# One stored batch of X instead of two: attention of odd batches split, w_out decoded later, GpSimd in pieces

## The chip, the cores and the metric

The kernel runs on one core of one Trainium2 chip. The metric is the device time of one execution in microseconds, as the median of several runs. Engines are named as in the profile: PE is TensorE's matrix multiplication and PEld its weight load, DVE is VectorE, ACT is ScalarE, POOL is GpSimd, SP is SyncE, which issues all DMAs here. "L227" is line 227 of the kernel.

## The reference

A linear attention without a softmax, normalised per head, feeds a gated block with a spatial mixing matrix. B = 8 batches, 8 heads, S = 576 positions, head size 64, d_model = 512, d_ff = 1024; everything is float32.

```python
kv  = einsum('bhsd,bhse->bhde', k, v)
o   = einsum('bhsd,bhde->bhse', q, kv)
x   = o / sqrt(mean(o*o, -1) + 1e-6) * g_norm          # then (b, s, h*d): 576 x 512
h   = maximum(x @ w_in, 0);  u, v = h[..., :512], h[..., 512:]
v_n = (v - mean(v)) / sqrt(var(v) + 1e-6)
v_s = einsum('ts,bsd->btd', w_spatial, v_n) + b_spatial[None, :, None]
out = (u * v_s) @ w_out
```

## The kernel before, in words

**Precision.** Products other than the attention's are made from high and low parts: a value is rounded to fp32r (the high part) and the rest is kept as a second fp32r tile, and each product is the sum of three matmuls, high x high, high x low and low x high (`hl`, `three`, L227). So there are pairs of tiles: XH/XL for the normalised attention output, WIH/WIL for w_in, VH/VL, WSH/WSL for w_spatial, GH/GL for the gated product, WOH/WOL for w_out. The inputs w_in and w_out come as 64-bit numbers and are decoded on the chip by `weight64` (L348 to L355): three ScalarE/VectorE steps for the high part, two VectorE steps for the rest, and two GpSimd instructions of 512 columns for the low part. The spatial weights are split by ScalarE and one GpSimd instruction of 640 columns (L378, L379).

**Stages of a batch.** 576 positions are four full tiles of 128 and a tail of 64. Two heads form a pair p (four pairs). For each pair: `att_k` (K, L110) makes K^T V in five matmuls and copies the two diagonal blocks to KVB, one by VectorE and one by ScalarE (L114, L115); `att_q` (Q, L165, L170) multiplies four Q tiles and the tail tile with it, and normalises the result (squares on ScalarE, sums on VectorE L151, a chain of five small VectorE instructions L127 to L135, a product L157); `att_t` (T, L195) transposes it on TensorE and splits it into XH and XL (L188, L189). `att_tail` does the same for the tail. Then come the hidden tiles `hv` (L258; relu, batch-norm statistics, normalisation, split into VH/VL; four per batch, and one tail tile for two batches), the gate tiles `u_unit` (eight of 288 columns), the spatial tiles `sp_unit` (eight of 288 columns, 14 matmuls each, with the gate multiplied in, L298 to L308), and the output tiles `out_unit` (four and a half per batch, L317 to L325).

**Two batches share a tail.** The tails of an even batch and the odd one behind it (64 rows each) form one tile of 128 rows. `hv_tail` makes its hidden tile and writes TA/TB, which every spatial tile of both batches needs for its last two matmuls (WTH, WTL). Before, XH and XL hold both batches side by side, each 1152 columns per pair, and the order of the spatial weights' columns differs between even and odd batches (`MAIN`, `WAT`, 640 stored columns of which an odd batch reads the tail columns first).

**Order.** The first part of the program is written out by hand in `PLAN`, one token a step: L asks for the next attention load, W for a weight load, C decodes the next weight tile (8 of w_in, 4 of w_spatial, 2 tails, 4 of w_out, in this order), J/K, D/A with B, T are steps of attention with their batch and pair, t, b, d those of a tail, H a quarter of a hidden tile, F its normalisation, h the tail's hidden tile, u, s, o gate, spatial and output tiles of batch 0, S one step of the queue. All attention of batch 1 and part of batch 2, and the decode of w_out, stand in it ahead of the first spatial tile. Behind PLAN a loop runs over batches 1 to 7: hidden, gate, spatial and output tiles; the 13 attention steps of batch b+2 are queued after the gate tiles of batch b, and `step()` takes one of them after each tile. A compile-time scheduler orders the instructions of each engine by priority (program order) and readiness in its own timing, so that an engine's order in the trace is not exactly the program's.

**Loads.** SP issues all loads in program order; a load waits there until its buffer is free. There are three buffers for keys and values and three for queries; `ahead`/`issue` keep at most three attention loads in flight. Weights come through two staging pools of five and four tiles; the space of one is used later for GH/GL, that of the other for WOH/WOL.

Of the kernel before, what the change touches and what calls it, by code (L numbers as in the profile page):

```python
# [19 lines left out]
P = 128  # L20
# [7 lines left out]
MAIN = (0, NT + 2 * TAIL)  # L28
TAILC = (NT, NT + TAIL)

WC = TAIL + S
WAT = (TAIL, 0)
# [4 lines left out]
N8 W L J00 D00 L W G J01 B00 C A01 L W L J02 T00 C H30 W B01 C D02 J03 H10 W C T01 L B02 C W  # L37
# [12 lines left out]
def body(ctx: ExitStack, tc, qT, kvlo, kvhi, g2, w_in, wsT, bsp, w_out, out):  # L50
# [19 lines left out]
    WSH = persistent([P, NC, WC], F32R, "WSH")  # L70
    WSL = persistent([P, NC, WC], F32R, "WSL")
    WTH = persistent([P, WC], F32R, "WTH")
    WTL = [persistent([P, WC], F32R, f"WTL{i}") for i in range(2)]
    XH = persistent([P, NP, 2 * S], F32R, "XH")
    XL = persistent([P, NP, 2 * S], F32R, "XL")
# [5 lines left out]
    KVB = [persistent([P, P], F32, f"KVB{i}") for i in range(2)]  # L81

# [7 lines left out]
    loaded = {}  # L90
    n_load = [0]

    def att_load(b, p):
        kv = KV[n_load[0] % 3]
        n_load[0] += 1
        for i, j in ((0, 2), (2, NC + 1)) if (b, p) == (0, 0) else ((0, NC + 1),):
            nc.sync.dma_start(kv[0:TAIL, :, i:j], kvlo[b, p, :, :, i:j])
            j = min(j, NC)
            nc.sync.dma_start(kv[TAIL:P, :, i:j], kvhi[b, p, :, :, i:j])
        qt = load.tile([P, S], F32, name="qt", tag="qt")  # L100
        nc.sync.dma_start(qt, qT[b, p])
        loaded[b, p] = kv, qt

    n_kv = [0]

    def att_k(b, p, st, copy=nc.vector.tensor_copy):
        kv, qt = loaded.pop((b, p))
# [4 lines left out]
        kvb = KVB[n_kv[0] % 2]  # L112
        n_kv[0] += 1
        copy(kvb[0:D, 0:D], ps[0:D, 0:D])  # L114
        nc.scalar.copy(kvb[D:P, D:P], ps[D:P, D:P])  # L115
        st[p] = kvb, qt
        issue()

# [42 lines left out]
    def att_qa(b, p, st, accumulate=False):  # L161
        kvb, qt = st[p]
        ps = ps_att.tile([P, 512], F32, name="pso", tag="att")
        for c in range(NC):
            nc.tensor.matmul(ps[:, c * P:(c + 1) * P], qt[:, c * P:(c + 1) * P], kvb,  # L165
                             start=True, stop=True)
        if p == 0:
            st["tail"] = ps_tail.tile([P, 512], F32, name="pst", tag="tail")

        nc.tensor.matmul(st["tail"][:, p * P:(p + 1) * P], qt[:, S - P:S], kvb,  # L170
                         start=True, stop=True)
# [19 lines left out]
    def att_t(b, p, st):  # L191
# [4 lines left out]
        cols = slice(MAIN[b % 2], MAIN[b % 2] + NT)  # L196
        split_x(ps, XH[:, p, cols], XL[:, p, cols])

# [8 lines left out]

    def att_steps(b):
        st = {}

        def t2():
            att_t(b, 2, st)
            tail_a(b, st)
            tail_b(b, st)

        K = lambda p: (lambda: att_k(b, p, st))
        Q = lambda p: (lambda: att_q(b, p, st))
        T = lambda p: (lambda: att_t(b, p, st))
        return [K(0), K(1), Q(0), K(2), Q(1), T(0), K(3), Q(2), T(1), Q(3), t2, T(3),
                lambda: att_tail(b, st)]  # L220
# [33 lines left out]
    def hv_k(b, c, k, ps):  # L254
        cols = slice(MAIN[b % 2] + c * P, MAIN[b % 2] + (c + 1) * P)
# [9 lines left out]
    def hv_tail():  # L265
        ps = ps_ho.tile([P, 512], F32, name="psh", tag="ho")
        cols = slice(NT, NT + 2 * TAIL)
# [10 lines left out]
    def u_unit(b, d, j):  # L278
        ps = ps_us.tile([P, 512], F32, name="psu", tag="us")
        cols = slice(j * HS, (j + 1) * HS)  # L280
        xs = slice(b % 2 * S + j * HS, b % 2 * S + (j + 1) * HS)
        fs = slice(d * P, (d + 1) * P)
        three(ps[:, 0:HS], [m for k in range(NP) for m in
                            hl(WIH[:, k, fs], WIL[:, k, fs], XH[:, k, xs], XL[:, k, xs])])
        nc.scalar.activation(U[:, d, cols], ps[:, 0:HS], AF.Relu)  # L285

    def sp_unit(b, d, j):
# [3 lines left out]
        ws = slice(WAT[i] + j * HS, WAT[i] + (j + 1) * HS)  # L291
        ds = slice(d * P, (d + 1) * P)
        pairs = [m for c in range(NC) for m in
                 hl(VH[:, c, ds], VL[:, c, ds], WSH[:, c, ws], WSL[:, c, ws])]
        pairs += [(TA[i][:, ds], WTH[:, ws]), (TB[i][:, ds], WTL[i][:, ws])]
# [3 lines left out]
        if i == 0:  # L299
            parts = [(slice(0, HS), cols)]  # L300
        elif j == 0:
            parts = [(slice(0, TAIL), slice(TAILC[1], TAILC[1] + TAIL)),
                     (slice(TAIL, HS), slice(0, HS - TAIL))]
        else:
            parts = [(slice(0, HS), slice(HS - TAIL, NT))]
# [23 lines left out]
    GH = GL = WOH = WOL = None  # L329
    staging = [ExitStack(), ExitStack()]  # L330
# [4 lines left out]
    def stage(i, n, dt=F32):  # L335
        pool = pools[1 if i < 4 else 0]
# [3 lines left out]
    def load64(src, i):  # L340
        nc.sync.dma_start(stage(i, 2 * DM, U32), src)

    def weight64(i, hi, lo):
# [10 lines left out]
        nc.gpsimd.tensor_tensor(f32(w1), f32(w1), f32(hi), op=ALU.subtract)  # L354
        nc.gpsimd.tensor_tensor(lo, f32(w1), f32(w0), op=ALU.add)  # L355
# [17 lines left out]
    def load_ws(c, i):  # L373
        nc.sync.dma_start(stage(i, WC), wsT[c * P:(c + 1) * P, :])

    def make_ws(c, i):
        t = staged.pop(i)
        nc.scalar.copy(WSH[:, c, :], t)  # L378
        nc.gpsimd.tensor_tensor(WSL[:, c, :], t, f32(WSH[:, c, :]), op=ALU.subtract)  # L379
# [5 lines left out]
    def load_tail(i, slot):  # L385

        rows, rest, h0, h1 = tail_rows(i)
        t = stage(slot, WC)
# [173 lines left out]
```

## Time and profile before

| | us |
|---|---|
| median of 3 runs | 553.45 (552.96 to 555.08) |
| profiled execution | 550.85 |
| its span in the profile | 549.1 |
| TensorE busy | 524.3 (95%) |
| VectorE busy | 312.6 (57%) |
| ScalarE busy | 220.1 (40%) |
| GpSimd busy | 51.8 (9%) |

The profile is one execution; its span starts with the first instruction and ends with the last, the rest of the 550.85 us lies around it. Busy times are unions over instructions; the engines work beside each other, so that their shares do not add up to 100%. A group's "mean ns" is the time from an instruction's start to its end; matmuls overlap, and 24 of 294 ns each can stand in 3.2 us. Idle time is put down to what ended it.

### The profile page before, as it was taken

The numbers are of one execution on the slowest core, as the hardware profiler recorded it, in microseconds if no ns is written. First come the engines' busy times: TensorE is split into PE (matmuls) and PEld (weight loads), VectorE is DVE, ScalarE is ACT, GpSimd is POOL, SyncE is SP. The second block draws the span as 40 slices with busy tenths as digits, with TensorE's granted clock in tenths as the row PEclk, the third lists the DMA queues.
The fourth block names the chain that finished last, engine by engine and source line by source line (L and its number), as shares of the span: only waits on it lengthen the run. The fifth ranks groups of instructions, "written<-read, shape, count | busy, mean of one in ns | idle before, by whom it ended". The sixth has DMA issues, their size and how long they took to land.

```text
span 549.1 us, 8840 instructions
## 1 busy us (share of the span) xinstructions
PE 524.3 (95%) x3344; PEld 480.0 (87%) x3344; DVE 312.6 (57%) x871; ACT 220.1 (40%) x576; POOL 51.8 (9%) x50
## 2 busy tenths in 40 slices
PE   7787978999999999999999999999999999999996
PEld 6666966988998889988999889988999889988995
DVE  1999999813565465555364465646546456314530
ACT  3766955422434343243433344334332434123312
POOL 6356643000000000000000000000000000000000
PEclk9999899999999999999999999999999999999999
DMA  8999835111244103430333202431100200010002
GB/s 227 288 278 227 271 90 140 33 39 39 69 104 125 59 0 89 112 116 20 87 88 84 100 1 65 109 108 55 44 23 1 78 20 1 0 47 32 1 1 96
DMA packets 20034, 46.26 MB, mean 84 GB/s; under 512 B 2644, under 2 KB 3156, under 8 KB 19992
## 3 DMA queue, kind: packets, MB, share of 16 engines
q1 hardware_dynamic: 19992, 45.70, 30.0%
q8 instruction: 26, 0.43, 0.3%
q14 instruction: 16, 0.13, 0.1%
HBM read 36.25 MB, written 9.44 MB: 83 GB/s over the span
## 4 chain that ended last, share of the span: by engine, by line
PE 82%; DVE 3%; ACT 0%; issue 0%; ACTq 0%; DVEq 0%
PE pss L227 21%; PE pso L227 18%; PE psu L227 16%; PE psh L258 14%; PE pskv L110 4%; PE pso L165 4%; PE pstr L195 2%; PE psh L227 1%; PE pst L170 1%; PE pstt L203 0%; DVE stage L353 0%; DVE ss L151 0%; DVE XL L189 0%; DVE x L157 0%; DVE rh L133 0%
## 5 line engine op out<-in xcount | busy, mean ns | idle before, releaser
L227 PE MATMUL pss<-WSH,VH 128*128 128x288 f32 x256 | 78.8, 308 | 1.3 <-DVE g L298 1.3
L227 PE MATMUL psu<-XH,WIH 128*128 128x288 f32 x256 | 77.6, 303 | 0.3 <-ACT U L285 0.3
L227 PE MATMUL psu<-XL,WIH 128*128 128x288 f32 x256 | 76.1, 298 | 0.0
L227 PE MATMUL psu<-XH,WIL 128*128 128x288 f32 x256 | 76.0, 298 | 0.0
L227 PE MATMUL pss<-WSH,VL 128*128 128x288 f32 x256 | 75.5, 295 | 0.0
L227 PE MATMUL pss<-WSL,VH 128*128 128x288 f32 x256 | 75.4, 295 | 0.0
L307 ACT CAST GH<-g 128x288 fp32r<-128x288 f32 (+2 forms) x80 | 29.0, 382 | 83.3 <-DVE g L298 83.2
L227 PE MATMUL pso<-WOH,GH 128*128 128x512 f32 x144 | 58.8, 408 | 0.4 <-ACT o L320 0.4
L227 PE MATMUL pso<-WOL,GH 128*128 128x512 f32 x144 | 56.8, 395 | 0.0
L227 PE MATMUL pso<-WOH,GL 128*128 128x512 f32 x144 | 56.8, 398 | 0.0
L237 DVE BATCH_NORM_STATS2 s<-v 128x6 f32<-128x512 f32 x36 | 24.8, 692 | 52.5 <-ACT v L234 52.5
L298 DVE TENSOR_TENSOR g<-pss,U 128x288 f32<-128x288 f32 x64 | 29.1, 456 | 44.8 <-PE pss L227 44.2
L258 PE MATMUL psh<-WIH,XH 128*128 128x512 f32 x128 | 51.0, 398 | 0.5 <-ACT XH L188 0.5
L227 PEld LDWEIGHTS psu<-XH,WIH 128*128 128x128 f32 x256 | 48.8, 191 | 1.5 <-ACT U L285 0.4
L258 PE MATMUL psh<-WIL,XH 128*128 128x512 f32 x128 | 50.1, 391 | 0.0
L227 PEld LDWEIGHTS pss<-WSH,VH 128*128 128x128 f32 x256 | 48.2, 188 | 2.0 <-DVE g L298 1.5
L227 PEld LDWEIGHTS psu<-XL,WIH 128*128 128x128 f32 x256 | 48.7, 190 | 1.2
L227 PEld LDWEIGHTS psu<-XH,WIL 128*128 128x128 f32 x256 | 48.7, 190 | 0.8
L258 PE MATMUL psh<-WIH,XL 128*128 128x512 f32 x128 | 48.6, 392 | 0.2 <-DVE XL L189 0.2
L110 PE MATMUL pskv<-KV 128*128 128x128 f32 x320 | 45.6, 282 | 3.2 <-DMA KV<-kvhi 3.0
L227 PEld LDWEIGHTS pss<-WSL,VH 128*128 128x128 f32 x256 | 48.2, 188 | 0.4
L227 PEld LDWEIGHTS pss<-WSH,VL 128*128 128x128 f32 x256 | 48.0, 188 | 0.0
(100 smaller groups left out, 982.0 us busy)
## 6 DMA issues: line engine op xcount, KB each, us to landing
KV<-kvlo SPq DMA_DIRECT2D x31, 320.0 KB, 4.5
qt<-qT SPq DMA_DIRECT2D x32, 288.0 KB, 3.9
out<-o SPq DMA_DIRECT2D x32, 256.0 KB, 2.0
KV<-kvhi SPq DMA_DIRECT2D x31, 256.0 KB, 4.0
stage<-w_in SPq DMA_DIRECT2D x8, 512.0 KB, 10.3
stage<-w_out SPq DMA_DIRECT2D x4, 512.0 KB, 6.6
stage<-wsT SPq DMA_DIRECT2D x4, 320.0 KB, 12.3
out<-o SPq DMA_DIRECT2D x8, 128.0 KB, 2.3
```

Of the source, the lines that this page charges most:

```text
L110: nc.tensor.matmul(ps[:, 0:P], kv[:, 0, c, :], kv[:, 1, c, :], start=c == 0, stop=c == NC)
L165: nc.tensor.matmul(ps[:, c * P:(c + 1) * P], qt[:, c * P:(c + 1) * P], kvb, start=True, stop=True)
L170: nc.tensor.matmul(st["tail"][:, p * P:(p + 1) * P], qt[:, S - P:S], kvb, start=True, stop=True)
L195: nc.tensor.transpose(ps[:, c * P:(c + 1) * P], x[:, c * P:(c + 1) * P], ident)
L227: nc.tensor.matmul(ps, lt, rh, start=i == 0, stop=i == n - 1)
L237: nc.vector.bn_stats(s6, v)
L258: nc.tensor.matmul(ps, lt, rh, start=k == 0 and i == 0, stop=k == NP - 1 and i == 2)
L298: nc.vector.tensor_tensor(g, ps[:, 0:HS], U[:, d, cols], op=ALU.mult)
L307: nc.scalar.copy(GH[:, d, dst], g[:, src])
```

## The change

XH and XL now hold one batch and both tails (640 columns per pair). An even batch's attention is queued as before. An odd batch's is cut in two: its four K^T V products, each followed at once by the matmul of the tail rows (`att_end`, with a small query tile of its own, qs), and the tail's normalisation are queued early, behind the even batch's steps; its main Q products, transposes and the copy of its tail columns into place (`move_tail`) are queued late, among the spatial tiles of the even batch. The odd batch's K^T V results are kept in four tiles KVO. Loads are of three kinds: f (all), k (keys, values and the tail's queries), q (the other queries). w_out's four tiles have a staging pool of their own and are loaded during batch 1's hidden tiles and decoded during batch 1's gate tiles; batch 0's output tiles follow behind those. GpSimd's instructions in `weight64`, `make_ws` and `make_tail` are cut into pieces of 128 columns. The spatial weights' columns are stored once, in natural order. The program's scratch area for dynamic DMAs is set to 1024 bytes.

```diff
-MAIN = (0, NT + 2 * TAIL)
+XC = NT + 2 * TAIL
 PLAN = """
...
-T02 H20 D03 H11 L L L W C L K10 B03 L C H00 T03 H21 d0 W H12 H22 b0 W H31 J11 t0 H01 D10 H13
-+ J12 W C W A11 B10 K13 C H23 u00 W A12 H32 A13 H02 W u01 u31 F1 u21 u30 u10 L C B11 W C W
-F2 W u20 B12 u11 H03 H33 W T11 d1 F3 S T10 T12 F0 S C C b1 C t1 W C B13 S C T13 h C C s30
-s31 s11 s21 s00 s20 s01 S s10 o1 S o3 S S S S S S o0 S o2
+H20 D03 H11 L L L W C L K10 B03 L C H00 T03 H21 d0 W H12 H22 b0 W H31 K11 t0 H01 H13 K12 W C W
+K13 d1 b1 C H23 u00 t1 W H32 H02 W W u01 u31 F1 u21 u30 u10 C C F2 u20 u11 H03 H33 F3 F0 C C h C m
+L A10 L s30 A11 B10 T10 s31 L s11 B11 T11 s21 L A12 s00 L B12 T12 s20 A13 s01 B13 T13 s10
-    XH = persistent([P, NP, 2 * S], F32R, "XH")
+    XH = persistent([P, NP, XC], F32R, "XH")
+    KVO = [persistent([P, P], F32, f"KVO{i}") for i in range(NP)]
     def att_k(b, p, st, copy=nc.vector.tensor_copy):
+        st[p] = KVO[p] if b % 2 else KVB[p % 2]
+        copy(st[p][0:D, 0:D], ps[0:D, 0:D])
+        nc.scalar.copy(st[p][D:P, D:P], ps[D:P, D:P])
+        if qs is not None:
+            att_end(p, st, qs)
+    def att_end(p, st, q):
+        if p == 0:
+            st["tail"] = ps_tail.tile([P, 512], F32, name="pst", tag="tail")
+        nc.tensor.matmul(st["tail"][:, p * P:(p + 1) * P], q, st[p], start=True, stop=True)
+    def move_tail():
+        to, of = (slice(c, c + TAIL) for c in TAILC)
+        nc.scalar.copy(XH[:, :, to], f32(XH[:, :, of]))
+        nc.gpsimd.tensor_copy(XL[:, :, to], f32(XL[:, :, of]))
     def att_steps(b):
+        if b % 2 == 0:
+            return [K[0], K[1], Q[0], K[2], Q[1], T[0], K[3], Q[2], T[1], Q[3], t2, T[3], end], []
+        return [loading(k) for k in K] + [tail, end], [Q[0], Q[1], T[0], Q[2], T[1], Q[3], T[2],
+                                                       T[3], move_tail]
     def sp_unit(b, d, j):
-        ws = slice(WAT[i] + j * HS, WAT[i] + (j + 1) * HS)
-        if i == 0:
+        if j == 0:
             parts = [(slice(0, HS), cols)]
         else:
+            n = NT - HS
+            parts = [(slice(0, n), slice(HS, NT)),
+                     (slice(n, HS), slice(TAILC[i], TAILC[i] + TAIL))]
+    stage_out = ctx.enter_context(tc.tile_pool(name="stage2", bufs=2))
+    def pieces(out, a, b, op):
+        for c in range(0, out.shape[-1], P):
+            e = min(c + P, out.shape[-1])
+            nc.gpsimd.tensor_tensor(out[:, c:e], a[:, c:e], b[:, c:e], op=op)
     def weight64(i, hi, lo):
-        nc.gpsimd.tensor_tensor(f32(w1), f32(w1), f32(hi), op=ALU.subtract)
-        nc.gpsimd.tensor_tensor(lo, f32(w1), f32(w0), op=ALU.add)
+        pieces(f32(w1), f32(w1), f32(hi), ALU.subtract)
+        pieces(lo, f32(w1), f32(w0), ALU.add)
+    todo = [(b + (kind != "f"), p, kind) for b in range(0, B, 2) for kind in "fkq"
+            for p in range(NP)]
     def first(b):
         for c in range(NC):
             hv(b, c)
             step()
+            if b == 1 and c < 2:
+                loads.pop(0)()
         for d in range(4):
-            if d == 3 and b % 2 == 0:
+            if d == 1 and b % 2 == 0:
                 step(len(queue))
                 hv_tail()
+            elif d == 2 and b % 2:
+                enqueue(b + 1)
+                enqueue(b + 2)
             for j in range(2):
                 u_unit(b, d, j)
                 step()
+            if b == 1:
+                conv()
+                if loads:
+                    loads.pop(0)()
+    first(1)
+    last(0)
+    second(1)
+    last(1)
+    for b in range(2, NB):
+        first(b)
+        if b % 2 == 0:
+            enqueue(b + 1, 1)
+        second(b)
+        last(b)
+        if b % 2 == 0:
+            step(len(queue))
```

`second(b)` holds the eight spatial tiles and `last(b)` the output tiles of a batch, each followed by one step of the queue.

## Rows read from the trace of the kernel before

**Rows 1.** The page's busy times: us, share of the span, instructions.
```profile
PE 524.3 (95%) x3344; PEld 480.0 (87%) x3344; DVE 312.6 (57%) x871; ACT 220.1 (40%) x576; POOL 51.8 (9%) x50
```
**Rows 2.** Busy times by stretch; last: granted clock, DMA share, GB/s.
```profile
core 0: us, PE busy (x) PEld busy (x) DVE busy (x) ACT busy (x) POOL busy (x), PEclk, DMA share, GB/s
0.00:46.00 46.00, 35.76 (x205) 30.78 (x205) 33.59 (x68) 27.17 (x107) 25.05 (x32) 1.00 1.00 259
46.00:96.00 50.00, 39.88 (x274) 37.14 (x272) 49.44 (x129) 33.48 (x98) 26.80 (x18) 0.93 0.65 179
110.00:530.00 420.00, 420.00 (x2694) 386.35 (x2693) 214.72 (x635) 149.88 (x349) 0.00 (x0) 1.00 0.20 56
```
**Rows 3.** Chain of waits in the saturated part: start, us, engine, tile, line, matmuls.
```profile
186.04 2.75 PE psh L258 x12
...
205.29 3.18 PE psu L227 x24
...
213.66 0.89 PE pso L165 x8
214.56 3.71 PE pss L227 x28
...
313.30 2.75 PE psh L258 x12
```
**Rows 4.** TensorE's waits before 110 us: waiter, released by, total us, times, longest.
```profile
PE pstt L203 <- DVE x L157: 3.6, 1, 3.6
...
PE pstr L195 <- DVE qh L128: 2.1, 1, 2.1
PE pstr L195 <- DVE x L157: 1.8, 1, 1.8
...
PE pso L165 <- ACT KVB L115: 1.0, 2, 0.5
```
**Rows 5.** TensorE in order of time, at 94 us: start, us, instruction.
```profile
94.02 0.40 PE L227 MATMUL pss<-WTH,TA 128*128 128x288 f32 x1 [0.30 <-DVE TA L276]
```
**Rows 6.** VectorE's groups, 46 to 95 us: count, busy us, mean ns, idle before.
```profile
L353 DVE SCALAR_TENSOR_TENSOR stage<-stage,t 128x512 f32<-128x512 uint32 x6 | 8.2, 1370 | 0.0
L151 DVE TENSOR_REDUCE ss<-sq 128x8 f32<-128x512 f32 x6 | 4.1, 676 | 0.0
L189 DVE SCALAR_TENSOR_TENSOR XL<-pstr,gcol,XH 128x512 fp32r<-128x512 f32 x5 | 3.7, 740 | 0.0
L350 DVE SCALAR_TENSOR_TENSOR stage<-stage,t 128x512 uint32<-128x512 uint32 x5 | 3.4, 682 | 0.0
L157 DVE TENSOR_TENSOR x<-pso,rh 128x512 f32<-128x512 f32 x5 | 3.4, 673 | 0.0
L127 DVE TENSOR_SCALAR ah<-ss 128x8 f32<-128x8 f32 x7 | 3.4, 480 | 0.0
...
L133 DVE TENSOR_TENSOR rh<-sh,qh 128x8 f32<-128x8 f32 x7 | 3.2, 461 | 0.3
...
L349 DVE TENSOR_SCALAR t<-t 128x512 uint32<-128x512 uint32 x4 | 2.5, 627 | 0.0
L135 DVE SCALAR_TENSOR_TENSOR rh<-qh,rh 128x8 f32<-128x8 f32 x7 | 2.1, 311 | 0.0
...
L134 DVE SCALAR_TENSOR_TENSOR qh<-sh,rh 128x8 f32<-128x8 f32 x7 | 1.9, 276 | 0.0
```
**Rows 7.** GpSimd: busy from 8 to 67 us, and its last instruction there.
```profile
8.00:67.00 59.00, 33.97 (x24) 0.97 1.00 265
...
65.24 1.56 POOL L405 TENSOR_TENSOR WTL<-stage,WTL 1x640 fp32r<-1x640 f32 x1 [0.97 <-ACT WTL L403]
```
**Rows 8.** GpSimd and VectorE near 19 us; VectorE's same group from 200 to 400 us.
```profile
18.45 1.55 POOL L354 TENSOR_TENSOR stage<-stage,WIH 128x512 f32<-128x512 f32 x1 [7.59 <-ACT WIH L351]
...
18.76 1.26 DVE L133 TENSOR_TENSOR rh<-sh,qh 128x8 f32<-128x8 f32 x1
...
L133 DVE TENSOR_TENSOR rh<-sh,qh 128x8 f32<-128x8 f32 x15 | 2.5, 165 | 1.1
```

More of the change, by code (lines that the diff above doesn't have):

```diff
@@ L161, in att_qa @@
     def att_qa(b, p, st, accumulate=False):
-        kvb, qt = st[p]
+        qt = queries.pop((b, p))
         ps = ps_att.tile([P, 512], F32, name="pso", tag="att")
         for c in range(NC):
-            nc.tensor.matmul(ps[:, c * P:(c + 1) * P], qt[:, c * P:(c + 1) * P], kvb,
+            nc.tensor.matmul(ps[:, c * P:(c + 1) * P], qt[:, c * P:(c + 1) * P], st[p],
                              start=True, stop=True)
[L167 to L171, printed above, removed]
+        if b % 2 == 0:
+            att_end(p, st, qt[:, S - P:S])
+        issue()
         st[p] = norm_a(ps, P, accumulate)
@@ L214, in t2, with tail @@
             tail_b(b, st)
[L216 to L220, printed above, removed]
+        def tail():
+            tail_a(b, st)
+            tail_b(b, st)
+        K = [lambda p=p: att_k(b, p, st) for p in range(NP)]
+        Q = [loading(lambda p=p: att_q(b, p, st)) for p in range(NP)]
+        T = [lambda p=p: att_t(b, p, st) for p in range(NP)]
+        end = lambda: att_tail(b, st)
+        if b % 2 == 0:
+            return [K[0], K[1], Q[0], K[2], Q[1], T[0], K[3], Q[2], T[1], Q[3], t2, T[3], end], []
+        return [loading(k) for k in K] + [tail, end], [Q[0], Q[1], T[0], Q[2], T[1], Q[3], T[2],
+                                                       T[3], move_tail]
     def three(ps, pairs):
@@ L404, in make_tail @@
         low = WTL[i][h1:h1 + 1]
-        nc.gpsimd.tensor_tensor(low, t[h1:h1 + 1], f32(low), op=ALU.subtract)
-    todo = [(b, p) for b in range(B) for p in range(NP)]
+        pieces(low, t[h1:h1 + 1], f32(low), ALU.subtract)
+    todo = [(b + (kind != "f"), p, kind) for b in range(0, B, 2) for kind in "fkq"
+            for p in range(NP)]
+    states = {}
     wanted = [0]
     def issue():
-        while wanted[0] and todo and len(loaded) < 3:
+        while wanted[0] and todo and (len(queries) if todo[0][2] == "q" else len(keys)) < 3:
             wanted[0] -= 1
@@ L436, in body, with enqueue @@
     queue = []
-    def enqueue(b):
-        for i, s in enumerate(att_steps(b)):
-            def go(i=i, s=s):
-                s()
-                if i in (2, 4, 7, 9):
-                    ahead()
-            queue.append(go)
+    def enqueue(b, late=0):
+        if b < NB:
+            queue.extend(att_steps(b)[late])
     def step(n=1):
@@ L478, in body @@
     psv += [ps_us.tile([P, 512], F32, name="psh", tag="us") for _ in range(2)]
-    st = [{}, {}]
+    st = [states.setdefault(b, {}) for b in range(2)]
     do = {
@@ L495, in body, with first @@
         do[token[0]](*map(int, token[1:]))
-    for b in range(1, NB):
+    def first(b):
         for c in range(NC):
```

103 lines of the change are left out of this document (51 added, 52 removed).

## The prediction

> **What bounds the kernel now.** I read the page's busy times first: TensorE is busy 524.3 of 549.1 us [rows 1], so at most 24.8 us can come from filling its gaps; the rest would need fewer or faster matmuls. The change leaves the list of matmuls as it is: the same 32 K^T V products, 32 main and 32 tail products with Q, 40 groups of four transposes, 36 hidden tiles, 64 gate tiles, 64 spatial tiles and 36 output tiles. Cutting the span into stages says where the gaps are [rows 2]: 10.2 us lie before 46 us, 10.1 us between 46 and 96 us, none from 110 to 530 us, and the rest at the very end (the last output tile and its store, untouched). In the second stretch the granted clock averages 0.93: of its 50 us another 3.5 us are lost at the lower level (1.2 GHz), after gaps of some us. So 46 to 96 us loses 10.1 + 3.5 = 13.6 us, and that is what the change can win or spoil.
>
> From there on TensorE is saturated. The chain of waits puts one hidden tile of an even batch at 186.04 us and the same tile of the next even batch at 313.30 us [rows 3]: 127.26 us for two batches, with no idle time of TensorE in them.
>
> What holds TensorE before 96 us is VectorE: it is busy 49.4 of 50 us [rows 2], and TensorE's largest wait is for rows that it normalises (3.6 us, [rows 4]). The gate to the saturated part is the first matmul on the pair's tail rows, at 94.02 us [rows 5]: once the tail tile of batches 0 and 1 is normalised, all spatial tiles of batch 0 can run.
>
> **What leaves the stretch before that gate.** VectorE's groups from 46 to 95 us [rows 6] hold work that the new order puts behind the gate:
> - w_out's decode, four of each form; of the three largest forms 4 x 1.37 + 4 x 0.68 + 2.5 = 10.7 us.
> - The main-tile normalisations of batch 1 and, in part, of batch 2: six sums of squares 4.1, five products x 3.4, five low parts XL 3.7, and six of the seven chains of small instructions, 6/7 x (3.4 + 3.2 + 2.1 + 1.9) = 9.1 us.
>
> Together 31 us by rows. The groups of this answer add to 59 us in 49 us of wall time, since neighbours overlap by some 0.08 us; scaled by 49/59 it is 26 us. The gate would open at 94 - 26 = 68 us. I add 1 us: GpSimd's weight instructions stay for the most part, so a wait that a removed small instruction bore can fall on its neighbour, against which stand two smaller forms that I have not counted. That gives 69 us. The spatial weights' low parts, which the gate also needs, end on GpSimd at 66.8 us [rows 7], so this is about as early as that side allows.
>
> **What TensorE has to do until 69 us.** Eight gate tiles at 3.18/2 = 1.59 us (12.7), the tail's hidden tile 2.75, the first two spatial tiles without their two tail matmuls 2 x 12/14 x 1.86 = 3.2, the last K^T V product and the tail matmuls some 2.4 (eight passes take 0.89) [rows 3]: 21 us in 23 us, with batch 1's Q products as filler if they are brought ahead. Not all can stand where the gap is; I allow 3 us idle and 1 us of low clock, 4 us lost.
>
> **What comes back later.** Batch 1's four Q products and transposes now stand between the spatial tiles, and batch 1's hidden tiles need the last of them; w_out is decoded during batch 1's gate tiles. From the gate to the first output tile TensorE has 11.6 (the rest of the spatial tiles) + 5.4 (four Q at 0.89 and transposes at half of it) + 11 (hidden) + 12.7 (gates) + 4.4 (batch 2) = 45 us. VectorE's usual mix is 214.7 of 420 us, 51% [rows 2], which makes 23 us, and the decode adds some 12: 35 of 45 us. It is covered, with less room than these stages have today; I put 1.5 us to the handover from the last transpose to the hidden tiles (0 to 4). The fourth w_out tile is the tight one. Its load waits until the second decoded tile has left its buffer (there are two), four VectorE and eight GpSimd steps follow, and the first output tile asks for it after nine matmuls, 9/12 x 2.75 = 2.1 us. Price 2 us, between 0 (decoded early) and 6 us (one whole chain: a row of before has 1.55 us for a GpSimd half of it [rows 8], and VectorE's four forms take up to 3.1 us by rows 6). Queued behind it are the output tiles on TensorE and, behind the load on SP, keys of batch 2, of which three tiles were asked for before.
>
> **The edits that I cost near nothing.** One X instead of two: a batch's transposes may write only after the gate tiles of the batch before have read; the new order has them behind those anyway, and an odd batch's last one, among the spatial tiles, has four output tiles (11 us) before its hidden tiles need it. One order of the spatial weights: 576 columns for 640 in six loads, and one more split per column block in even batches, 16 pairs of small copies in stages where VectorE is half idle. The move of the tail stands between output tiles; nobody asks for it before the next gate tiles. The separate query loads: 16 more issues on SP, which has no work of its own; batch 1's large ones leave the first stretch, where the DMA share is 1.00 [rows 2], worth 0 to 2 us there, which I leave to the range.
>
> The odd batches' tail matmul is the exception: it follows its own K^T V product and waits for both copies of it. The row of before for such a wait is 0.5 us [rows 4]; 16 of them cost 0 to 8 us. TensorE's order in the trace is not the program's (passes of one product stand apart, with gate tiles between them), so something ready usually fills the wait. I take 0.6 us in all.
>
> **GpSimd in 128 columns.** No row has such an instruction. GpSimd runs one 512-column subtraction from 18.45 to 20.00 us, and VectorE's 8-column product that starts at 18.76 takes 1.26 us and ends with it, while its undisturbed mean is 0.165 us [rows 8]: it waits for all of that instruction. This waiting is why the small forms of rows 6 take 0.28 to 0.48 us. Cut in four, one wait is shorter, but each of the four can hold another VectorE instruction up; with VectorE saturated I take zero, between 5 us won and 5 us lost (below). On GpSimd a piece is 1.55/4 = 0.39 us, and each may first let a VectorE instruction of up to 0.7 us pass.
>
> The Trainium skill ("SBUF — State Buffer", "SBUF: two separate sides") says that the port pair shared by these two engines is locked for a whole instruction and that the loser blocks fully; the 1.26 us agree. By that rule a shorter instruction means a shorter block, and the first rival is what it would make of this kernel. The skill's "GPSIMD Engine Reference" ("Instruction dispatch") speaks against the edit: every GpSimd instruction is broadcast and looked up in software before its loop starts, so four pieces pay this four times; by it the third rival gains. No row here shows either price for a piece.
>
> **Sum.** Lost from 46 us on: before 13.6; after 4 + 1.5 + 2 + 0.6 = 8.1. Gain 5.5 us. The profiled execution took 550.85 us, so 545.4 us on its terms; it lies 2.6 us under the median of the timed runs, 553.45, and what will be measured is a median: 553.45 - 5.5 = 548.0 us.
>
> **Rivals.**
> - Short GpSimd pieces free VectorE. Of the idle time before 46 us at least 2.1 + 1.8 us follow VectorE [rows 4]; half of it, and 2.5 us between 46 us and the gate, come on top: 543.5 us. For it: the 1.26 us row. Against: two engines that take turns lose the same in sum.
> - The gap is only moved. The tail's own chain (product, squares, transposes, hidden tile, normalisation) is serial, the gate opens at 75 us (8 us lost), w_out's chain costs 4, the handover 1: 13.6 - (8 + 4 + 1 + 0.6) = 0, 553.5 us. That w_out's decode still runs ahead of the gate, so that the change does not do what it says, would end here too. For it: VectorE's work is deferred, not removed.
> - Slower: GpSimd becomes the bound of the weights. From 8 to 67 us it is busy 34 of 59 us [rows 7], a slack of 25 us. The change adds 80 instructions there (48 for w_in, 32 for spatial weights and tails); each with a start of its own and a VectorE instruction let by, they decide from 25/80 = 0.31 us each on. At 0.4 us they need 32 us: the weights come 7 us late at the gate, and with 3 us more gaps from w_in's low parts before 46 us (8.1 + 7 + 3) - 13.6 = 4.5 us are lost, 558 us. Against it: VectorE's instructions that read PSUM seem not to be held up (x takes 0.67 us in rows 6), so GpSimd can work beside them.
>
> **How the numbers follow.** Forecast 548.0 (545.5 to 551) 0.42, freed VectorE 0.20, moved gap 0.17, slower 0.21. Runs of this kernel can tell 0.5%, 2.8 us, from no change. Faster by more than that: 0.42 x 0.88 + 0.20 = 0.57. Within: 0.05 + 0.14 = 0.19. Slower: 0.21 + 0.03 (the moved gap with dearer chains) = 0.24. For 8 in 10 the range reaches from 541.5 (freed VectorE and the 2 us of the loads) to 558.
>
> **What would show it.** Right: the first matmul on tail rows near 69 instead of 94 us; TensorE idle for under 5 us between 46 us and there; two batches again 127.3 us apart; no 8-column VectorE instruction of 1.26 us, though as much waiting in sum; w_out's decode beside batch 1's gate tiles. Wrong: that matmul after 76 us, GpSimd without idle time ahead of it, TensorE's waits for the copies of K^T V in late batches, or a gap of over 4 us ahead of the first output tile.

## The result and the profile after

| | before | after |
|---|---|---|
| median, same chip, 4 runs each | 553.97 us (552.96 to 555.08) | 547.6 us (545.47 to 549.9) |
| ratio | | 0.9885, 95% interval 0.9838 to 0.9932 |
| profiled execution / its span | 550.85 / 549.1 us | 548.28 / 546.5 us |
| the change repeated on another chip | 552.96 us | 547.67 us, ratio 0.9901 (0.9887 to 0.9914) |

The change makes the kernel 1.0 to 1.2% faster; 548.0 us had been forecast. The two profiled executions show only 549.1 - 546.5 = 2.6 us of it: that of before ran 3.1 us under the median of its runs here, that of after 0.7 us over its own. From that spread I estimate that a stage read from one profile is good to about 3 us, so the verdicts below come from the ratios (each against runs of the kernel before on the same chip), and the rows only say where.

The page's busy times of after, beside [rows 1]:

```profile
PE 525.5 (96%) x3344; PEld 482.3 (88%) x3344; DVE 300.2 (55%) x890; ACT 221.8 (41%) x579; POOL 77.8 (14%) x162
```

TensorE's list is the same length. GpSimd has gone from 51.8 to 77.8 us and from 50 to 162 instructions. After by stretches (the columns of [rows 2]):

```profile
0.00:46.00 46.00, 36.08 (x197) 31.23 (x197) 30.43 (x73) 27.29 (x107) 34.72 (x75) 0.89 1.00 263
46.00:96.00 50.00, 43.45 (x278) 40.33 (x277) 42.08 (x114) 30.44 (x80) 39.45 (x80) 0.90 0.46 116
96.00:130.00 34.00, 34.00 (x230) 31.83 (x229) 18.07 (x62) 13.42 (x33) 2.39 (x6) 1.00 0.29 74
130.00:530.00 400.00, 400.00 (x2594) 369.74 (x2593) 208.09 (x639) 147.54 (x354) 1.20 (x3) 1.00 0.23 62
```

From 46 to 96 us TensorE now idles 6.6 us, not 10.1, and VectorE is busy 42.1 us, not 49.4. From 96 to 530 us TensorE has no idle time; before it had 0.1 us there.

TensorE in order of time, after: start, us, instruction, idle time before it and what ended it. The answers to [rows 5]:

```profile
53.36 2.48 PE L115 MATMUL pskv<-KV 128*128 128x128 f32 x10 [3.53 <-DMA KV<-kvlo]
...
58.43 0.77 PE L128 MATMUL pst<-KVO,qs 128*128 128x128 f32 x2 [0.39 <-DMA qs<-qT]
...
66.15 0.60 PE L211 MATMUL pstt<-ident,x 128*128 128x128 f32 x4
66.58 1.95 PE L176 MATMUL pso<-KVO,qt 128*128 128x128 f32 x16
...
83.49 0.29 PE L252 MATMUL pss<-WTH,TA 128*128 128x288 f32 x1
...
85.61 0.40 PE L252 MATMUL pss<-WSH,VH 128*128 128x288 f32 x1 [0.97 <-DVE g L321]
```

The gate, the first matmul on tail rows, stands at 83.49 us (82.41 us in the repetition): 10.5 us earlier than before, where 25 had been forecast. It is a serial chain that ends there, which begins with the odd batch's last K^T V product at 53.36 us. The fourth of these rows is part of what TensorE did meanwhile: two Q products of batch 1 (eight passes each). VectorE's part of the chain, after:

```profile
64.92 0.69 DVE L168 TENSOR_TENSOR x<-pst,rh 128x512 f32<-128x512 f32 x1
...
70.66 0.48 DVE L198 SCALAR_TENSOR_TENSOR XL<-pstt,gcol,XH 128x256 fp32r<-128x256 f32 x1 [0.88 <-ACT XH L197]
...
76.83 0.68 DVE L262 BATCH_NORM_STATS2 s<-v 128x6 f32<-128x512 f32 x1
...
81.31 1.41 DVE L301 TENSOR_TENSOR TA<-v,TA 64x512 fp32r<-64x512 f32 x2
```

Product, normalisation, transposition, hidden tile, statistics and TA follow one another over 30 us, through TensorE, ScalarE and VectorE in turn. From the last product of tail rows (58.43 us) to the gate it is 25.1 us; the repetition has 25.8 us (56.65 to 82.41).

GpSimd in after from 53 us on (start, us, instruction):

```profile
53.66 2.16 POOL L370 TENSOR_TENSOR stage<-stage,WOH 128x128 f32<-128x128 f32 x4
...
56.14 2.38 POOL L370 TENSOR_TENSOR stage<-stage,WOH 128x128 f32<-128x128 f32 x4
...
59.02 4.87 POOL L370 TENSOR_TENSOR WSL<-stage,WSH 128x128 fp32r<-128x128 f32 x10
```

It works almost without a break until 78.6 us and then stands idle to 88.9 us. Two w_out tiles (WOH) are still decoded here, ahead of the gate: their loads were issued at 35 us, since the tiles of the new staging pool were free and the scheduler drew them forward. The other two were decoded behind the gate, as planned.

The small instructions of VectorE, 46 to 90 us, after (count, busy us, mean ns, idle before), beside [rows 6]:

```profile
L146 DVE SCALAR_TENSOR_TENSOR rh<-qh,rh 128x8 f32<-128x8 f32 x4 | 1.0, 258 | 0.0
L144 DVE TENSOR_TENSOR rh<-sh,qh 128x8 f32<-128x8 f32 x4 | 0.9, 233 | 0.2
L145 DVE SCALAR_TENSOR_TENSOR qh<-sh,rh 128x8 f32<-128x8 f32 x4 | 0.8, 197 | 0.0
```

Their means were 311, 461 and 276 ns; the longest of these forms in the whole profile takes 0.46 us, none 1.26 us any more.

### The profile page after: what moved, and what is told of

Read it like the earlier page. It is cut to its first block, busy times and chain, and to the rows that moved or that the text cites. A ratio compares the mean times of both kernels' runs of the same rounds, so it can differ in the third digit from the quotient of the medians.

```text
span 546.5 us, 9007 instructions
## 1 busy us (share of the span) xinstructions
PE 525.5 (96%) x3344; PEld 482.3 (88%) x3344; DVE 300.2 (55%) x890; ACT 221.8 (41%) x579; POOL 77.8 (14%) x162
## 3 DMA queue, kind: packets, MB, share of 16 engines
q1 hardware_dynamic: 22296, 46.06, 31.3%
## 4 chain that ended last, share of the span: by engine, by line
PE 85%; DMA 10%; DVE 3%; ACT 1%; SPq 1%; issue 0%; DVEq 0%; ACTq 0%
PE pss L252 21%; PE pso L252 19%; PE psu L252 17%; PE psh L283 14%; PE pskv L115 5%; DMA KV<-kvhi 5%; PE pso L176 4%; DMA qt<-qT 4%; PE pstr L204 2%; PE psh L252 2%; DMA qs<-qT 1%; PE pst L128 1%; ACT WTL L432 0%; PE pstt L211 0%; DVE XL L198 0%
## 5 line engine op out<-in xcount | busy, mean ns | idle before, releaser
L262 DVE BATCH_NORM_STATS2 s<-v 128x6 f32<-128x512 f32 x36 | 24.8, 692 | 69.8 <-ACT v L259 69.6
L252 PE MATMUL pso<-WOH,GH 128*128 128x512 f32 x144 | 58.4, 407 | 0.7 <-ACT o L342 0.7
L329 ACT CAST GH<-g 128x64 fp32r<-128x64 f32 (+2 forms) x96 | 30.4, 349 | 61.2 <-DVE g L321 61.0
L220 POOL CAST XL<-XL 128x256 fp32r<-128x256 f32 x4 | 1.6, 400 | 360.7 <-DVE rh L144 254.5
L115 PEld LDWEIGHTS pskv<-KV 128*128 128x128 f32 x320 | 42.3, 203 | 8.8 <-issue 3.7
```

The source lines that it names most:

```text
L220: nc.gpsimd.tensor_copy(XL[:, :, to], f32(XL[:, :, of]))
L252: nc.tensor.matmul(ps, lt, rh, start=i == 0, stop=i == n - 1)
L262: nc.vector.bn_stats(s6, v)
L329: nc.scalar.copy(GH[:, d, dst], g[:, src])
```

## The experiments

Which part carries the gain? Four kernels make a square: the new order and the short GpSimd pieces, each with and without the other.

| | whole GpSimd instructions | 128-column pieces |
|---|---|---|
| order of before | 1 | 0.9948 (0.9919 to 0.9978) |
| order of after | 1.0095 (1.0059 to 1.0132) | 0.9901 (0.9887 to 0.9914) |

**The new order with whole instructions.** In `pieces`:

```diff
-        for c in range(0, out.shape[-1], P):
-            e = min(c + P, out.shape[-1])
-            nc.gpsimd.tensor_tensor(out[:, c:e], a[:, c:e], b[:, c:e], op=op)
+        nc.gpsimd.tensor_tensor(out, a, b, op=op)
```

> The changed kernel with GpSimd's instructions whole again (512 or 576 columns). Theory (pieces are neutral for VectorE in sum): GpSimd's busy time falls from 78 to 50 us, VectorE's 8-column instructions of 1.2 us come back, the time stays within 2 us of 547.6. Rival 1 (short pieces free VectorE): 551 to 554 us, the gate two to four us later. Rival 2 (pieces make GpSimd the bound of the weights): 542 to 545 us, the gate earlier by 2 us or more.

557.8 us, ratio 1.0095 (1.0059 to 1.0132), slower than before and more than any of the three accounts allowed; the gate stands at 96.91 us. Its stretch:

```profile
46.00:96.00 50.00, 34.25 (x204) 31.33 (x202) 43.11 (x93) 28.71 (x72) 24.99 (x20) 0.90 0.46 113
```

GpSimd there, in order of time:

```profile
59.98 1.49 POOL L368 TENSOR_TENSOR WOL<-stage 128x512 fp32r<-128x512 f32 x1
61.42 1.40 POOL L368 TENSOR_TENSOR WSL<-stage,WSH 128x576 fp32r<-128x576 f32 x1
62.79 1.03 POOL L368 TENSOR_TENSOR WOL<-stage 128x512 fp32r<-128x512 f32 x1
```

And VectorE beside it:

```profile
58.63 1.93 DVE L380 SCALAR_TENSOR_TENSOR stage<-stage,t 128x512 f32<-128x512 uint32 x1
60.48 0.99 DVE L145 SCALAR_TENSOR_TENSOR qv<-sv,rv 128x1 f32<-128x1 f32 x1
61.40 1.44 DVE L146 SCALAR_TENSOR_TENSOR rv<-qv,rv 128x1 f32<-128x1 f32 x2
62.76 2.88 DVE L266 TENSOR_SCALAR v<-v,mv,rv 128x512 f32<-128x512 f32 x2
```

GpSimd's instructions follow back to back, and VectorE's end with them: the product at 60.48 us at 61.47 with the second, the two behind it at 62.84 with the third (62.82). Six VectorE instructions, three of them of one column, take 58.6 to 65.6 us. VectorE is busy 43.1 us there with 93 instructions; in after 42.1 us with 114. So a busy time of VectorE contains its waits. TensorE idles 15.75 us in the stretch. The rest of the change alone costs 1%, and the pieces turn it into a gain.

**The old order with pieces.** The kernel before, with `pieces` in its five GpSimd calls:

```diff
-        nc.gpsimd.tensor_tensor(f32(w1), f32(w1), f32(hi), op=ALU.subtract)
-        nc.gpsimd.tensor_tensor(lo, f32(w1), f32(w0), op=ALU.add)
+        pieces(f32(w1), f32(w1), f32(hi), ALU.subtract)
+        pieces(lo, f32(w1), f32(w0), ALU.add)
```

> The kernel before with only GpSimd's instructions cut into 128 columns. Neutral pieces: 552 to 555 us, as before. Short pieces free VectorE: 547 to 550 us. GpSimd as the bound of the weights: 556 to 560 us, GpSimd without idle time from 20 to 70 us.

550.37 us, 0.9948 (0.9919 to 0.9978). Its stretch:

```profile
46.00:96.00 50.00, 39.35 (x266) 35.52 (x264) 40.66 (x115) 31.57 (x81) 39.73 (x83) 0.93 0.69 181
```

And its gate:

```profile
94.02 0.40 PE L227 MATMUL pss<-WTH,TA 128*128 128x288 f32 x1 [0.30 <-DVE TA L276]
```

VectorE is busy 40.7 us of this stretch instead of 49.4, and the gate stands where it was. Its profiled execution and that of before are equally long (550.88 and 550.85 us), so the rows don't show where the half per cent of the medians lies. If the two parts simply added, both together would stand at 0.9948 + 1.0095 - 1 = 1.0043; they stand at 0.9901. The other 1.4% (8 us) come only from having both.

**Is it the width?** The step of the loop in `pieces` set to 256 and to 64:

```diff
-        for c in range(0, out.shape[-1], P):
-            e = min(c + P, out.shape[-1])
+        for c in range(0, out.shape[-1], 2 * P):     # and P // 2
+            e = min(c + 2 * P, out.shape[-1])
```

> The changed kernel with GpSimd's pieces 256 columns wide instead of 128. Theory (each VectorE instruction that needs both its operands from SBUF waits for the one GpSimd instruction in progress, so that the cost goes with the length of a GpSimd instruction times the number of VectorE's, not with GpSimd's total): between the changed kernel and the whole instructions (1.0095), at 0.991 to 0.998, VectorE's chain members up to 0.75 us. Rival (the 128 columns won because another order of the instructions came out of the compile-time scheduler): no order by width, 256 may lie anywhere from 0.985 to 1.01 while the chain members are 0.75 us all the same.

> The kernel after with GpSimd's pieces 64 columns wide in place of 128. The microbenchmark's streams alone give a start of 0.11 us and 0.31 us per 128 columns for one GpSimd instruction (0.41 us at 128 columns, 1.33 at 512), so a 64-column piece should take some 0.26 us and eight of them 2.1 us instead of 1.66. Theory (a VectorE instruction waits for one GpSimd instruction, and VectorE is what holds TensorE): the waits halve again, from some 0.25 to 0.15 us each, and the ratio goes on down from 0.990 to 0.98 to 0.988; the first tail-row matmul stands before 82 us. Rival (GpSimd is now the bound of the weights): it has no idle time from 20 to 30 and from 40 to 60 us with 128-column pieces already, so 0.4 us more for each of some 30 old instructions ahead of the tail's spatial weights puts 5 to 12 us on the gate (88 to 95 us): ratio 0.995 to 1.005, though the small instructions' waits are shorter.

| columns | ratio | gate, us | last product of tail rows to gate, us | GpSimd busy 46 to 96 us |
|---|---|---|---|---|
| whole | 1.0095 (1.0059 to 1.0132) | 96.9 | 35.3 | 25.0 |
| 256 | 1.0003 (0.9988 to 1.0019) | 94.1 | 29.4 | 34.0 |
| 128 | 0.9901 (0.9887 to 0.9914) | 82.4 | 25.8 | 39.5 |
| 64 | 0.9945 (0.9922 to 0.9969) | 81.9 | 29.1 | 49.5 |

Down to 128 columns each halving is worth a per cent, and the chain to the gate gets shorter with each. At 64 the 1-column products of VectorE fall further (0.18 us in the mean, 0.38 at 128 columns in the repetition), but one 8-column product waits far longer than for one piece. GpSimd's row and VectorE's product:

```profile
64.54 9.38 POOL L370 TENSOR_TENSOR WSL<-stage,WSH 128x64 fp32r<-128x64 f32 x30
70.68 3.32 DVE L144 TENSOR_TENSOR rh<-sh,qh 128x8 f32<-128x8 f32 x1 [1.09 <-ACT sh L137]
```

The product ends at 74.00 us, with that row of thirty pieces (73.92 us), some ten pieces after it began; it stands ahead of the tail's statistics on VectorE. So a wait isn't always bounded by one piece, which neither account had; why this one product didn't get in between was not settled. TensorE has a new wait too. Its waits before 130 us at 64 columns:

```profile
PE psu L252 <- POOL WIL L370: 6.2, 2, 3.9
PE psh L283 <- POOL WIL L370: 3.2, 1, 3.2
```

That is 9.4 us for w_in's low parts, of which the repetition of after has 1.7: here GpSimd is a bound, as the rival had it, but not at the gate, which it had at 88 to 95 us.

**The price by itself.** A kernel that computes nothing of the reference: chains of twelve 8-column VectorE products, alone and beside 6 x 512 GpSimd columns, whole or as 24 pieces; then six 512-column VectorE products in place of the chain (`wide`).

```diff
+        if width:
+            for _ in range(6):
+                for c in range(0, 512, width):
+                    nc.gpsimd.tensor_tensor(z[:, c:c + width], x[:, c:c + width],
+                                            y[:, c:c + width], op=ALU.mult)
+        for _ in range(small):
+            nc.vector.tensor_tensor(s, s, e8, op=ALU.mult)
+        for _ in range(wide):
+            nc.vector.tensor_tensor(w, w, y, op=ALU.mult)
```

> A kernel that computes nothing of the reference (its output is zeros): chains of 12 dependent 8-column VectorE products, alone and beside 3072 columns of GpSimd products, as six instructions of 512 or 24 of 128 columns; then six VectorE products of 512 columns beside the same. Theory (one wait per VectorE instruction): the chain alone takes 12 x 0.2 = 2.4 us; beside whole instructions six of its members wait about 1.1 us each, so about 8 us; beside pieces all 12 wait up to 0.35 us each, 5 to 6.5 us, though GpSimd's stream is as long. Rival (sum conserved): the chain is as long beside pieces as beside whole instructions. GpSimd's stream alone: 24 pieces cost 6.5 to 9 us against 6 to 6.5 us for six whole ones; beside six VectorE products of 0.69 us it grows by up to 0.69 us per instruction it must wait for.

VectorE's chains in order of time, alone, beside whole instructions and beside pieces (start, us of all twelve, instruction):

```profile
3.91 2.37 DVE L82 TENSOR_TENSOR s<-s,e 128x8 f32<-128x8 f32 x12 [1.40 <-ACT s L75]
28.55 7.55 DVE L82 TENSOR_TENSOR s<-s,e 128x8 f32<-128x8 f32 x12 [22.27 <-ACT s L75]
38.10 4.74 DVE L82 TENSOR_TENSOR s<-s,e 128x8 f32<-128x8 f32 x12 [2.00 <-ACT s L75]
```

GpSimd's streams, whole and in pieces, first alone and then beside the chain:

```profile
7.50 7.97 POOL L79 TENSOR_TENSOR z<-x,y 128x512 f32<-128x512 f32 x6 [7.06 <-ACT x L73]
16.70 9.94 POOL L79 TENSOR_TENSOR z<-x,y 128x128 f32<-128x128 f32 x24 [1.22 <-ACT x L73]
27.86 8.02 POOL L79 TENSOR_TENSOR z<-x,y 128x512 f32<-128x512 f32 x6 [1.22 <-ACT x L73]
37.41 9.95 POOL L79 TENSOR_TENSOR z<-x,y 128x128 f32<-128x128 f32 x24 [1.53 <-ACT x L73]
```

Beside whole instructions the chain loses 7.55 - 2.37 = 5.2 us, beside pieces 2.4 us, though the pieces keep GpSimd busy longer. GpSimd loses nothing to the chain (7.97 and 8.02, 9.94 and 9.95): of these 8-column products VectorE bears all of the waiting. One start of a piece costs (9.94 - 7.97)/18 = 0.11 us.

It is otherwise beside 512-column VectorE products. GpSimd's streams, whole and in pieces, and the three rows of six such products:

```profile
50.46 9.60 POOL L79 TENSOR_TENSOR z<-x,y 128x512 f32<-128x512 f32 x6 [3.11 <-ACT x L73]
61.29 13.98 POOL L79 TENSOR_TENSOR z<-x,y 128x128 f32<-128x128 f32 x24 [1.23 <-ACT x L73]
49.08 8.19 DVE L84 TENSOR_TENSOR w<-w,y 128x512 f32<-128x512 f32 x6 [6.24 <-ACT w L74]
58.06 5.95 DVE L84 TENSOR_TENSOR w<-w,y 128x512 f32<-128x512 f32 x6 [0.79 <-ACT w L74]
64.80 5.20 DVE L84 TENSOR_TENSOR w<-w,y 128x512 f32<-128x512 f32 x6 [0.79 <-ACT w L74]
```

Here GpSimd waits as well: its pieces take 13.98 us in place of 9.94, its whole instructions 9.60 in place of 7.97. The products ran over from one stretch into the next, so none of them was timed alone and a price per product can't be read off; in the last row each takes 0.82 to 0.90 us, where the first one of all, which began before GpSimd's stream, takes 0.69 us.

**Which pieces?** Pieces of 128 columns in the decode of w_in alone, or in the spatial weights, tails and w_out alone; and, last, 128 columns in w_in with 64 in the others (the edit is cut to its main lines):

```diff
-        for c in range(0, out.shape[-1], P):
+        for c in range(0, out.shape[-1], width[0]):
     def make_in(half, k, i):
+        width[0] = 128      # 576 in the second, 128 in the third kernel
     def make_out(k, i):     # make_ws, make_tail the same
+        width[0] = 576      # 128 in the second, 64 in the third kernel
```

> The kernel after with 128-column pieces in the decode of w_in alone; the spatial weights, the tails and w_out are made by whole GpSimd instructions. Theory (the pieces pay where VectorE's chain of the tail stands before the gate, from 46 us on): this keeps little of the gain: TensorE loses 12 to 16 us between 46 and 96 us as with whole instructions, ratio 1.000 to 1.010. Rival (the pieces pay wherever VectorE and GpSimd run together, in proportion to GpSimd's work: 16 of the 34 old instructions are w_in's and all of those stand before 60 us): half of the gain, 0.997 to 1.002, with TensorE's share of 0 to 46 us as in the kernel after (36.1 to 36.5 us).

> The kernel after with 128-column pieces in the spatial weights, the tails and w_out, and whole GpSimd instructions in the decode of w_in. Theory (the pieces pay where the tail's chain stands before the gate): most of the gain stays, ratio 0.988 to 0.995, TensorE loses 6 to 9 us between 46 and 96 us, and what is lost lies before 46 us (TensorE below 35.5 us there). Rival (in proportion to GpSimd's work): half of the gain, 0.997 to 1.002, with the gate later than 88 us.

w_in alone: 556.58 us, 1.0081 (1.0049 to 1.0113), gate 92.1 us. The others alone: 553.16 us, 1.0012 (0.9989 to 1.0034), gate 89.6 us. Their stretches, w_in alone first:

```profile
46.00:96.00 50.00, 37.37 (x212) 33.81 (x211) 43.71 (x99) 27.20 (x71) 28.18 (x29) 0.83 0.38 102
```

```profile
46.00:96.00 50.00, 37.87 (x237) 34.87 (x236) 41.89 (x112) 29.45 (x75) 36.57 (x71) 0.90 0.42 107
```

From 1.0095 the one set wins 0.14%, the other 0.83%, both 1.94%. Neither account fits both kernels: the theory (only what stands beside the tail's chain pays) holds for w_in alone and misses the other, proportion the reverse. The larger share does lie with the instructions beside the chain. From the last product of tail rows to the gate it is 30.8 us with w_in's pieces alone (from 61.31 us) and 31.3 us with the others alone (from 58.28 us), between the 35.3 us of neither and the 25.8 us of both; so each set shortens the chain by about half of what both do, but why w_in's pieces pay in time only when the others are cut too was not settled.

> The kernel after with 128-column pieces in the decode of w_in and 64-column pieces in the spatial weights, the tails and w_out. With 64 columns everywhere TensorE waits 9.4 us for the low parts of w_in (WIL, three waits), while VectorE's 1-column instructions of the hidden tiles take 0.18 to 0.21 us in place of 0.24 to 0.38. Theory (narrow pieces pay where VectorE's chain stands before the gate, and cost where GpSimd stands before TensorE): the waits for WIL go, the shorter 1-column instructions stay, and the ratio falls below that of the kernel after: 0.983 to 0.990, gate at 78 to 83 us. Rival (GpSimd bounds the spatial weights and the tails as well, since it has no idle time from 40 to 60 us): 18 more pieces for the four spatial weights, 20 for the tails and 16 for each w_out tile, at 0.1 us each, move the gate back by as much as VectorE wins: 0.990 to 0.996, with TensorE waiting for WSL or WTL, or the gate after 84 us.

550.47 us, 0.995 (0.9924 to 0.9977), gate 85.6 us: no better than 64 columns everywhere, worse than 128. The waits for w_in's low parts are gone, as the theory had it. But these are among TensorE's largest waits before 130 us:

```profile
PE pskv L115 <- DMA KV<-kvlo: 5.5, 2, 3.6
...
PE pst L128 <- DMA qs<-qT: 2.7, 2, 2.3
```

The size is the rival's, but TensorE waits for keys and queries, not for spatial weights, so its mechanism isn't shown either: the chain to the gate is as long as with 128 columns (26.0 us), but it begins later (59.62 us). No version tried beats the kernel after.

**Do the two early w_out tiles hold the gate?** The first two w_out loads are made to wait for TA:

```diff
-        load64(w_out[k * P:(k + 1) * P, :], i)
+        t = stage(i, 2 * DM, U32)
+        if k < 2:
+            nc.scalar.copy(f32(t[:, 0:1]), f32(TA[0][:, 0:1]))
+        nc.sync.dma_start(t, w_out[k * P:(k + 1) * P, :])
```

> The changed kernel, but the first two w_out loads wait for the pair's tail hidden tile (one ScalarE copy of a TA column into the load's buffer is put in front). Theory (loads): in the changed kernel two w_out loads of 0.5 MB each were issued at 35 us, in the stretch where the DMA share is 1.05, ahead of batch 1's last keys; TensorE waited 3.5 us for these and then ran at the lower clock until 62 us. Held back, that wait is under 1 us, the granted clock of 50 to 60 us is 0.9 or more instead of 0.63, the first tail-row matmul comes at 79 to 80 instead of 83.5 us, and the time is 542 to 544 us against 547.6. Rival (the tail's serial chain and GpSimd hold the gate): the keys come earlier but the gate stays at 82 to 84 us and the time within 1 us of 547.6. Second rival (w_out comes back as a wait): a gap of over 2 us ahead of the first output tile, 548 to 551 us.

549.75 us, 0.9934 (0.9908 to 0.996): no gain. Its gate:

```profile
81.57 0.29 PE L252 MATMUL pss<-WTH,TA 128*128 128x288 f32 x1
```

TensorE's largest wait in it (total, times, longest):

```profile
PE pstt L211 <- DVE x L168: 5.9, 1, 5.9
```

The last K^T V product came at 47.2 us instead of 53.4, and GpSimd was busy 30.5 us instead of 39.5 in the stretch; yet the gate moved by 2 us, and TensorE lost 5.9 us in front of the tail's transposes. The chain began earlier (last product of tail rows at 54.02 us instead of 58.43) and less decode beside it did not shorten it: 27.6 us to the gate, 25.1 in after.

The same with whole instructions:

```diff
+        nc.gpsimd.tensor_tensor(out, a, b, op=op)    # in pieces, and the hold as above
```

> Both edits: w_out's loads held back and GpSimd's instructions whole. If the two costs are independent, the time is the changed kernel's plus the sum of the two differences: loads theory with neutral pieces 542 to 544 us; with pieces that free VectorE 546 to 549; with GpSimd as bound 537 to 541.

558.28 us, 1.0108 (1.0067 to 1.015), gate 88.07 us. None of the sums expected was near it. The gate comes 8.8 us earlier than with whole instructions alone: the chain begins 4.0 us earlier (57.65 us) and is 4.9 us shorter (30.4 us). But 6.7 us of idle time appear between 96 and 130 us, where a transposition waits 5.8 us for VectorE.

**Is the late decode worth anything?** All four w_out tiles loaded and decoded ahead of the gate (of the edit only the plan is shown; the four staging tiles and the steps taken out behind the gate are not):

```diff
-K13 d1 b1 C H23 u00 t1 W H32 H02 W W u01 u31 F1 u21 u30 u10 C C F2 u20 u11 H03 H33 F3 F0 C C h C m
+K13 d1 b1 C H23 u00 t1 W H32 H02 W W W W W W u01 u31 F1 u21 u30 u10 C C F2 u20 u11 H03 H33 F3 F0 C C C C C C h C m
```

> The changed kernel with all four w_out tiles loaded and decoded ahead of the gate (four buffers for them): the part of the change that defers w_out undone. In the changed kernel the scheduler pulled two of the four ahead anyway. Theory (work taken from VectorE and GpSimd ahead of the gate is what opens it earlier): two tiles more cost 2 x 2.2 us of VectorE and 2 x 3.9 us of GpSimd there, gate 4 to 8 us later, 3 to 6 us slower than the changed kernel (0.995 to 1.000). Rival (the serial chain of the tail holds the gate, and VectorE and GpSimd have room): within 1.5 us of the changed kernel.

551.32 us, 0.9963 (0.9947 to 0.998). TensorE's largest wait before 130 us, its last product of tail rows and the gate:

```profile
PE pskv L115 <- DMA KV<-kvlo: 5.8, 2, 5.4
...
62.82 0.39 PE L128 MATMUL pst<-KVO,qs 128*128 128x128 f32 x2
...
88.07 0.40 PE L252 MATMUL pss<-WTH,TA 128*128 128x288 f32 x1 [0.77 <-DVE TA L301]
```

Two tiles behind the gate are worth 0.9963 - 0.9901 = 0.6%, 3.4 us. The size is the theory's, but not the way: from 62.82 us to the gate the chain takes 25.3 us, as in after (25.1), so the work of the decode didn't lengthen it. It begins 4.4 us later, behind the last keys. With no, two and four w_out loads issued ahead of these keys TensorE waits 1.2, 3.5 (1.7 in the repetition) and 5.4 us for them, and the last product of tail rows stands at 54.0, 58.4 (56.7) and 62.8 us. By these rows it is w_out's loads, more than their decode, that put the gate off here.

**The change again**, on another chip:

> The changed kernel once more, in the company of the two below, to have its ratio to the kernel before on one chip with theirs: 0.985 to 0.993 (0.9885 so far).

547.67 us, 0.9901 (0.9887 to 0.9914).

Every edit here also changes the order that the compile-time scheduler gives each engine; the 5.9 us wait above is an example. This is worth a few us and was not separated. The price measured by itself doesn't rest on it, and the row of four widths, of which three fall in one line, rests on it least.

## Why the prediction was right, and where its steps were wrong

The time came within 0.4 us, but not by the sum that was given.

- **The pieces at zero: wrong, and the step that matters.** "With VectorE saturated I take zero" and "two engines that take turns lose the same in sum" do not hold. In the new order the pieces are worth 1.94%, some 10.5 us, and they alone decide between 1.0095 and 0.9901. A small VectorE instruction waits for the GpSimd instruction that is running, and GpSimd loses nothing to it; so the sum of the waits goes with the length of one GpSimd instruction, not with GpSimd's work (5.2 against 2.4 us for the same columns). Beside 512-column VectorE products GpSimd loses too (13.98 against 9.94 us), so there the two do take turns. The saturation itself was the misreading: in the 49.4 of 50 us of [rows 2] these waits are counted as busy; the old order with pieces has 40.7. The Trainium skill's rule of the locked port ("SBUF — State Buffer", "SBUF: two separate sides") had been cited there and outvoted; the rows at 512 and 128 columns agree with it, the 3.32 us product at 64 columns waited for longer than one instruction. The first rival, 0.20, had this mechanism; its time, 543.5 us, was 4 us too low.
- **The gate at 69 us: wrong.** It stands at 83.5 and 82.4 us; the second rival, with its serial chain, had 75. Taking 26 us of VectorE's work off 94 us treats the gate as the end of VectorE's work. It is the end of a chain through three engines: the two held w_out tiles, work of the same kind, moved it by 2 us only, and in the old order with pieces VectorE's busy time fell by 8.8 us while the gate stayed at 94.02 us. Of the prediction's own marks for "wrong" one was met, that matmul after 76 us; another was met in part, as GpSimd had no idle time from 40 to 65 us but 5 us just ahead of the gate.
- **Lost until the gate, 3 us idle and 1 us of low clock: too little.** From 46 to 96 us it was 6.6 us idle, 5.6 of them ahead of the gate, and the granted clock was 0.90, which by the prediction's own reckoning is 50 x 0.10 = 5.0 us. The stretch with a low clock follows the wait for keys (53.36 us):

```profile
50.00:55.00 5.00, 1.64 (x8) 1.67 (x9) 4.54 (x12) 2.08 (x6) 5.00 (x9) 0.76 0.98 204
55.00:60.00 5.00, 3.65 (x15) 3.07 (x15) 3.74 (x11) 3.43 (x14) 5.00 (x10) 0.50 0.84 233
```

  A clock of 0.50 is the level of 1.2 GHz. A gate 14 us late cost no more, as TensorE had Q products, transposes and, from 81.1 us, hidden matmuls of batch 1 to do; the Q products had been named as filler "if they are brought ahead".
- **What comes back later, 1.5 + 2 + 0.6 us: nothing of it came.** From 85.6 to 530 us TensorE has no idle time, neither at the handover, nor ahead of the first output tile (121.05 us), nor for the copies of K^T V. With the terms measured so the ledger reads 13.6 - 11.6 = 2.0 us. It leaves out that the granted clock before 46 us fell from 1.00 to 0.89, and a share of a stretch at the lower level isn't all lost, since TensorE partly waits there anyway. Over the whole span TensorE's idle time fell from 24.8 to 21.0 us, 3.6 of it between 46 and 96 us, and its busy time rose from 524.3 to 525.5 us: that makes the 2.6 us between the two spans. The 5.3 to 6.4 us of the medians are larger; the profile of before was one of its quicker executions, and what the others lose was not seen.
- **The saturated part is unchanged: right.** The tails' hidden tiles of two successive pairs of batches, beside [rows 3]:

```profile
322.69 2.30 PE psh L252 x10
...
450.02 2.30 PE psh L252 x10
```

  127.33 us apart, 127.26 before.
- **w_out late: half right.** Two of four tiles were, for 3.4 us, which by the rows above came from their loads more than from their decode; that the other two could slip forward, because the program's order puts no bound on a free buffer, stood only among the rivals.
- **GpSimd as the bound: wrong at 128 columns, right in part at 64.** A 128-column piece of 128 rows takes 0.43 to 0.72 us in the mean beside VectorE (0.47 alone, with a new one every 0.41; 0.39 estimated), and GpSimd had no idle time from 40 to 65 us, but TensorE waits for w_in's low parts 0.3 us only (1.7 in the repetition). The start of an instruction that the Trainium skill's "GPSIMD Engine Reference" ("Instruction dispatch") describes costs 0.11 us a piece here; it shows in TensorE's waits at 64 columns.

So the number came out by two errors that cancelled: some 10 us of gain set to zero, against a new order that is not 5.5 us faster by itself but 5.3 slower.

## What to carry to other kernels

Where VectorE's short instructions run beside GpSimd, the length of one GpSimd instruction sets what they wait, and VectorE's busy time hides it: read the means of its small forms against undisturbed ones before calling it saturated. Cut GpSimd's work until the cuts make it the bound (of four widths 128 columns was best here; 64 was too far). For a gate, follow the chain that ends at it, link by link, and read its start and its length apart: loads moved the start here, GpSimd's width the length. Work taken off a busy engine moves the gate only as far as that work stood in the chain.

## What the runs showed of the hardware

Beside back-to-back GpSimd instructions of 512 columns, two 8-column VectorE products got in per GpSimd instruction (12 in 7.55 us, at 1.33 us each), beside 128-column pieces one (12 in 4.74 us, at 0.41 us each), and GpSimd was not slowed by either. Beside 512-column VectorE products GpSimd was slowed: 24 pieces took 13.98 us instead of 9.94, six whole instructions 9.60 instead of 7.97. Beside 64-column pieces one 8-column product waited 3.32 us, over some ten pieces.
